# Attention and a gated MLP on one core: a list schedule for the opening only, later chunks emitted in a loop over inner tiles

## The chip, the cores and the metric

The kernel runs on 1 core of one Trainium2 chip. A core has five engines that work side by side, each through its own queue in order: PE (TensorE: matrix products), DVE (VectorE), ACT (ScalarE), POOL (GpSimd) and SP (SyncE, here only for starting transfers). PEld is PE's loading of weights, which overlaps its products. ACT and POOL start transfers too, from their own queues. The metric is the device time of one execution in microseconds (us), the median of several runs. The profile adds the span of one profiled execution, and the clock that PE was granted, as a share of full speed.

## The reference

Two stages, all in float32. The first is attention over 8 batches x 8 heads x 576 positions x 64: a coarse part (q, k and v averaged over groups of 4 positions, full attention over the 144 averages, each result used 4 times) plus a local part (each position sees the 7 positions at a distance under 4). The second is RMS-norm and a gated MLP over the 4608 tokens of 512 values.

```python
q_d, k_d, v_d = (t.reshape(B, H, S // 4, 4, D).mean(axis=3) for t in (q, k, v))
out_up = np.repeat(sm_attn(q_d, k_d, v_d), 4, axis=2)

mask = np.abs(pos[:, None] - pos[None, :]) < 4
scores = np.where(mask, scale * np.matmul(q, k.transpose(0, 1, 3, 2)), -1000000000.0)
out_local = np.matmul(softmax(scores), v)

x = (out_up + out_local).transpose(0, 2, 1, 3).reshape(4608, 512)
xn = x / np.sqrt(np.mean(x * x, axis=-1, keepdims=True) + 1e-06) * rms_g
g = xn @ w_gate                                  # 512 -> 1536
out = (g / (1 + np.exp(-g)) * (xn @ w_val)) @ w_out   # 1536 -> 512
```

## The kernel before

**Tiles and stages.** The 4608 tokens are cut into 18 chunks of 256 (`c`, `NCH`), each as two tiles of 128 (`j`); a token is one position of one batch, its 512 values are 8 heads x 64. The inner width 1536 is cut into 12 inner tiles of 128 (`f`, `NF`). Three classes hold the work.

`Coarse` is one step of the coarse attention: a pair of heads of one batch, 32 steps in all. PE makes the scores (L462), DVE takes their maximum (L471), ACT the exponentials (L481), PE turns them (L490), ACT copies, PE multiplies by the values (L504), DVE scales, and a transfer puts the result into DRAM. The sums over 4 positions behind it are made by `Sums` with accumulating transfers: SP fetches the first quarter, POOL issues three that add the others, for `qk` and for `vs` (L352).

`Attention(c)` is the local attention of chunk c, up to the operand of the MLP. Eight score products of 896 columns, each with a sum (DVE, L669 and L673), a softmax over 7 places (the exponential on ACT, L696; the rest on DVE, L700 to L707), eight value products whose 7 places are shared out among ACT (L716), DVE and POOL (both L723), and their sums (DVE, L742). Then the coarse results are fetched (`load_up`, transfers from ACT's queue) and added, ACT squares and sums (L767), PE makes the mean (L774), DVE starts an inverse root, POOL makes three Newton rounds of four instructions on 128x8 values (L799 to L802), and DVE multiplies (`norm`, L806). Last comes what this document calls the turn: PE transposes (L818, 4 for each half of the chunk), ACT copies the result as `xh` (L822), and DVE takes the remainder as `xl` (L826). `xh` and `xl` are the high and low halves of x, so that three fast products stand for one of float32.

`Forward(c)` is the MLP of a chunk. For each f: 24 first products (L870; 12 for the gate, 12 for the value, each xh and xl against high and low weights that stay in the core's memory), a tanh (ACT, L877), `gate` and `product` (DVE, L880 and L885), the high half `hs` of the result (ACT, L891) and its low half (`low`, L894), and two inner tiles later (`LAG`) 6 second products of 512 columns (L905). At the end of a chunk ACT copies two output tiles (L912) and SP stores them.

**What sets the order.** `Plan` is a list scheduler that runs while the program is built. Each piece of work is a task with an engine, an estimated cost, a due time (`due[c]` is when chunk c is to begin) and the buffers that it uses. Again and again it takes the engine that can begin first, and among the tasks that this engine could begin by then the one with the earliest due time, and emits it. Coarse steps are spread out over three stretches of time by due times. Some tasks have two engines to choose from; `low` is one:

```python
low = task(
    (("DVE", 0.42, soon), ("POOL", 0.95, soon)), 0, lambda e, f=f: self.low(f, e), soon, [high], uses=[sil, hs],
)
```

The plan's own clock goes to the end of the kernel. Up to 270 us of it the order of emission is the order of the program, word for word (`manual_schedule`); what is emitted later is put in order once more by the framework's own scheduler, with the order of emission as its priority.

```python
plan.start()
with tc.manual_schedule():
    plan.run(270.0)
plan.run()
```

**The opening.** Until the first MLP can begin, the core loads and splits the weights (`decode`, on SP, ACT, POOL and DVE), makes eight coarse steps and the attention of chunks 0 and 1, whose value sums go to PE. Eight more coarse steps follow from `due[1] + 10` on, due 18.4 us apart on the plan's clock.

Of the kernel before, what the change touches and what calls it, by code (L numbers as in the profile page):

```python
# [167 lines left out]
def attn_moe_kernel(  # L168
# [135 lines left out]
    def load_second(f):  # L304
# [19 lines left out]
    class Sums:  # L324


        def __init__(self, b, half, at):
# [97 lines left out]
    class Coarse:  # L425


        def __init__(self, b, hp, at, pool=None, tag="ps_a", after=()):
# [22 lines left out]
            stored[b, hp] = task("ACT", 0.06, self.store, at, [scaled], uses=[og], lag=2.2)  # L451

        def scores(self):
# [375 lines left out]
    class Forward:  # L829


        def __init__(self, att, weights, second_weights):
# [132 lines left out]
    def first_weights(f):  # L965
# [12 lines left out]
    atts = [Attention(0, 1, 2, (ps_o, "ps_o"), "DVE")]
    atts.append(Attention(
        1, 2, 2, (ps_a, "ps_a"), "DVE", [h.valued for h in opening] + atts[0].turns,  # L980
    ))
    for p_, (t0, t1) in enumerate(((due[1] + 10, due[4] - 30), (due[4], due[9] - 35), (due[9], due[13] - 35))):
        n = 2 * KT * (p_ + 1)
        for i, it in enumerate(coarse[n:n + 2 * KT]):
            Coarse(*it, t0 + (t1 - t0) * i / 7, after=atts[1].added if p_ == 0 else ())
    for c in range(2, NCH):
        atts.append(Attention(c))
# [83 lines left out]
```

## Time and profile before

| | |
|---|---|
| median of 3 runs | 1203.33 us (1202.26 to 1211.03) |
| the profiled execution | 1203.4 us |
| its span in the trace | 1201.6 us |
| mean granted clock of PE in it | 0.962 |
| first product of chunk 0 | 106.5 us after the span's start |

Each row of the page's first part gives an engine's busy time, its share of the span and its instructions. A row of the windows gives, after the stretch and its length, each engine's busy time in it with the number of its instructions, the granted clock, the busy share of the transfer engines and what they moved. In the timeline and the chain of waits stand the time of the start in us, the duration, the engine, what it made, the line and how many instructions were put together; what follows in square brackets is how long the engine had stood idle ahead of it and who released it. In the table of waits stand PE's instruction, the arrow to the instruction that it waited for, and then the sum, the number and the longest of these waits.

The costliest groups of instructions on PE and on DVE, with busy time and mean duration (ns), then the idle time ahead of them and what ended most of it (products overlap on PE, so the mean of one is longer than the time from one to the next):

```profile
L870 PE MATMUL ps_h<-xh,wg 128*128 128x256 f32 x1728 | 357.4, 289 | 5.0 <-DVE sil L885 2.0
L673 DVE TENSOR_REDUCE sc<-prod 128x14 f32<-128x896 f32 x144 | 153.9, 1076 | 0.6
```

### The profile page before, as it was taken

The numbers are of one execution on the slowest core, as the hardware profiler recorded it, in microseconds if no ns is written. First come the engines' busy times: TensorE is split into PE (matmuls) and PEld (weight loads), VectorE is DVE, ScalarE is ACT, GpSimd is POOL, SyncE is SP. The second block draws the span as 40 slices with busy tenths as digits, with TensorE's granted clock in tenths as the row PEclk, the third lists the DMA queues.
The fourth block names the chain that finished last, engine by engine and source line by source line (L and its number), as shares of the span: only waits on it lengthen the run. The fifth ranks groups of instructions, "written<-read, shape, count | busy, mean of one in ns | idle before, by whom it ended". The sixth has DMA issues, their size and how long they took to land. (4 is left out here: it accounts for less than half of the span.)

```text
span 1201.6 us, 22370 instructions
## 1 busy us (share of the span) xinstructions
PE 1117.7 (93%) x8002; PEld 1021.3 (85%) x8002; DVE 894.0 (74%) x1638; ACT 628.2 (52%) x2284; POOL 370.1 (31%) x590
## 2 busy tenths in 40 slices
PE   5875799999799889999899999999999999999998
PEld 4774688888688788989889998989999999999997
DVE  6786898787884879798796388989585978983232
ACT  1664663747454737557274274664555564672121
POOL 1653451334232233324322234241212222242000
PEclk8866799999899999999999999999999999999999
DMA  9985382446365244263524234543040313300000
GB/s 264 301 281 152 83 207 70 91 94 134 90 126 102 76 93 118 66 137 77 132 55 115 39 91 102 127 88 95 26 111 25 106 52 88 98 12 18 1 18 19
DMA packets 76816, 119.59 MB, mean 100 GB/s; under 512 B 26784, under 2 KB 36256, under 8 KB 76704
## 3 DMA queue, kind: packets, MB, share of 16 engines
q1 hardware_dynamic: 47520, 97.34, 27.7%
q0 software_dynamic: 8640, 15.93, 8.9%
q10 hardware_dynamic: 20544, 4.89, 1.9%
q8 instruction: 63, 1.03, 0.4%
q14 instruction: 49, 0.40, 0.1%
HBM read 106.33 MB, written 11.80 MB: 98 GB/s over the span
## 5 line engine op out<-in xcount | busy, mean ns | idle before, releaser
L905 PE MATMUL ps_o<-wo,hs 128*128 128x512 f32 x1296 | 361.4, 403 | 20.8 <-POOL hs L894 13.2
L870 PE MATMUL ps_h<-xh,wg 128*128 128x256 f32 x1728 | 357.4, 289 | 5.0 <-DVE sil L885 2.0
L870 PE MATMUL ps_h<-xh,wv 128*128 128x256 f32 x1728 | 348.1, 286 | 6.5 <-DVE sil L880 3.9
L870 PEld LDWEIGHTS ps_h<-xh,wg 128*128 128x128 f32 x1728 | 288.9, 194 | 18.2 <-DVE sil L885 3.4
L870 PEld LDWEIGHTS ps_h<-xh,wv 128*128 128x128 f32 x1728 | 283.9, 192 | 16.5 <-DVE sil L880 6.1
L716 ACT ACTIVATE prod<-kv,sc 128x64 f32<-128x64 f32 x1072 | 282.9, 404 | 19.6 <-DVE sc L707 9.8
L905 PEld LDWEIGHTS ps_o<-wo,hs 128*128 128x128 f32 x1296 | 225.8, 192 | 59.3 <-POOL hs L894 15.8
L870 PE MATMUL ps_h<-xl,wg 128*128 128x256 f32 x864 | 247.2, 286 | 0.3 <-DVE xl L826 0.2
L870 PE MATMUL ps_h<-xl,wv 128*128 128x256 f32 x864 | 245.1, 284 | 0.0
L894 POOL TENSOR_TENSOR hs<-sil,hs 128x256 fp32r<-128x256 f32 x124 | 109.7, 896 | 263.3 <-ACT hs L891 250.9
L877 ACT ACTIVATE sil<-ps_h 128x256 f32<-128x256 f32 x216 | 82.3, 381 | 206.4 <-PE ps_h L870 150.6
L891 ACT ACTIVATE hs<-sil 128x256 fp32r<-128x256 f32 x216 | 87.8, 413 | 190.6 <-DVE sil L885 180.8
L870 PEld LDWEIGHTS ps_h<-xl,wg 128*128 128x128 f32 x864 | 167.8, 194 | 5.5 <-DVE xl L826 1.0
L870 PEld LDWEIGHTS ps_h<-xl,wv 128*128 128x128 f32 x864 | 166.0, 192 | 3.9
L669 DVE TENSOR_TENSOR prod<-q_t,kv 128x896 f32<-128x896 f32 x140 | 156.3, 1123 | 5.6 <-DMA q_t<-in_q_band_dram 5.2
L723 POOL TENSOR_TENSOR prod<-sc,kv 128x256 f32<-128x256 f32 x144 | 113.8, 822 | 141.6 <-DVE x_t L742 100.5
L742 DVE TENSOR_REDUCE x_t<-prod 128x128 f32<-128x896 f32 x128 | 137.4, 1078 | 26.7 <-POOL prod L723 12.2
L880 DVE SCALAR_TENSOR_TENSOR sil<-sil,ps_h 128x256 f32<-128x256 f32 x216 | 89.4, 414 | 87.5 <-ACT sil L877 45.0
L673 DVE TENSOR_REDUCE sc<-prod 128x14 f32<-128x896 f32 x144 | 153.9, 1076 | 0.6
L885 DVE SCALAR_TENSOR_TENSOR sil<-sil,ps_h 128x256 f32<-128x256 f32 x216 | 89.3, 416 | 78.6 <-PE ps_h L870 77.7
L723 DVE TENSOR_TENSOR prod<-sc,kv 128x128 f32<-128x128 f32 (+2 forms) x144 | 70.8, 516 | 1.4 <-DMA kv<-in_v_pad_dram 0.5
L352 POOL DMA_DIRECT2D qk<-in_qk_sum_dram x36 | 32.4, 901 | 118.1 <-DMA qk<-in_qk_sum_dram 88.7
(118 smaller groups left out, 1034.3 us busy)
## 6 DMA issues: line engine op xcount, KB each, us to landing
kv<-in_k_pad_dram SPq DMA_DIRECT2D x72, 320.0 KB
kv<-in_v_pad_dram SPq DMA_DIRECT2D x72, 320.0 KB
qk<-in_qk_sum_dram POOLq DMA_DIRECT2D x36, 288.0 KB, 4.6
out_dram<-o_sb SPq DMA_DIRECT2D x36, 256.0 KB
q_t<-in_q_band_dram SPq DMA_DIRECT2D x70, 128.0 KB
vs<-in_v_sum_dram POOLq DMA_DIRECT2D x36, 144.0 KB, 3.7
qk<-in_qk_sum_dram SPq DMA_DIRECT2D x12, 288.0 KB
wo<-in_qk_sum_dram SPq DMA_DIRECT2D x2, 1152.0 KB
```

The costliest lines, as they stand in the source:

```text
L669: nc.vector.tensor_tensor(out=pr, in0=bcast(q[:, s0:s0 + 2], 2, NO), in1=window(k, s0), op=ALU.mult)
L673: nc.vector.tensor_reduce(out=self.sc[:, j, par, s0:s0 + 2], in_=self.pr[i], axis=AX.X, op=ALU.add,)
L716: nc.scalar.activation(out=self.pr[i][:, o, s], in_=self.v[j, par][:, s0 + s + o], func=AF.Copy, scale=p[:, s, o:o + 1],)
L723: (nc.vector if engine == "DVE" else nc.gpsimd).tensor_tensor(out=self.pr[i][:, a:b], in0=bcast(p[:, :, a:b].rearrange("p s o -> p o s"), ...
L742: nc.vector.tensor_reduce(out=self.x[j][:, s0:s0 + 2, par], in_=pr.rearrange("p o s d -> p s d o"), axis=AX.X, op=ALU.add,)
L870: nc.tensor.matmul(out=self.p[f][:, t], lhsT=wi(f)[:, 0, k], rhs=xi[:, k], start=(n == 0), stop=(n == 3 * KT - 1),)
L877: nc.scalar.activation(out=self.sil[f], in_=self.p[f][:, 0], func=AF.Tanh, scale=0.5)
L880: nc.vector.scalar_tensor_tensor(out=self.sil[f], in0=self.sil[f], scalar=1.0, in1=self.p[f][:, 0], op0=ALU.add, op1=ALU.mult,)
L885: nc.vector.scalar_tensor_tensor(out=self.sil[f], in0=self.sil[f], scalar=0.5, in1=self.p[f][:, 1], op0=ALU.mult, op1=ALU.mult,)
L891: nc.scalar.activation(out=self.hs[f][:, 0], in_=self.sil[f], func=AF.Copy)
L894: (nc.gpsimd if engine == "POOL" else nc.vector).tensor_tensor(out=self.hs[f][:, 1], in0=self.sil[f], in1=self.hs[f][:, 0], op=ALU.subtract,)
L905: nc.tensor.matmul(out=self.o[j], lhsT=lhs[:, cols], rhs=rhs(f)[:, 0], start=(f == 0 and i == 0), stop=(f == NF - 1 and i == 2),)
```

## The change

**Three numbers.** `FIRST` = 3, `EARLY` = 7, `COARSE` = {3: 1}. The plan now holds only the opening's tasks: the attention of chunks 0 to 3, the MLP of chunks 0 to 2, the splitting of the weights, and after the first eight coarse steps only `EARLY` = 7 more, due 14 us apart from `due[1] + 10` on. It runs under `manual_schedule` until `due[3] + 10` = 247 us of its own clock.

**A loop for the rest.** The constructors that made tasks are now methods `plan`, and next to them stand methods that emit the same instructions without the plan: `emit(f)` and `emit_second(f)` of `Forward`, `steps()` of `Attention` and of `Coarse`. For chunks 3 to 17 a loop runs over f. Each round emits the inner tile's first products and what follows on ACT and DVE, then the second products of two inner tiles earlier, then those steps of chunk c+1's attention and of the next coarse steps whose place (a number between 0 and 12, in inner tiles) has come. There are two coarse steps to a chunk, in chunk 3 one, until all 32 are made. What the loop emits is ordered once more by the framework's scheduler.

```diff
+        def emit(self, f):
+            self.first(f, 0)
+            self.first(f, 1)
+            self.tanh(f)
+            self.gate(f)
+            self.product(f)
+            self.high(f)
+            self.low(f, "DVE")
+
+        def emit_second(self, f):
+            self.second(f)
+            if f == NF - 1:
+                for j in range(2):
+                    self.copy(j)
+                    self.store(j)
```

So `low` goes to DVE throughout from chunk 3 on; in the plan's chunks it still has its choice. The places of the attention steps (each function emits the lines named above; `root` goes from the mean to `norm`):

```diff
+            todo = [(0.37 * i, lambda i=i: score(i)) for i in range(8)] + [(3.0, softmax)]
+            todo += [(3.1 + 0.42 * i, lambda i=i: value(i)) for i in range(8)]
+            todo += [(at, lambda j=j: add(j)) for j, at in enumerate((4.8, 6.4))]
+            return todo + [(6.5, root), (10.4, lambda: turn(0)), (10.5, lambda: turn(1))]
```

A coarse step is emitted in two parts, `low` (the sums' transfers where they are due, the scores to the exponentials) and `high` (the turning to the store), 1.2 inner tiles apart:

```diff
     plan.start()
     with tc.manual_schedule():
-        plan.run(270.0)
+        plan.run(due[FIRST] + 10)
     plan.run()
+    att, late = atts[FIRST], []
+    for c in range(FIRST, NCH):
+        todo = []
+        if c + 1 < NCH:
+            nxt = Attention(c + 1)
+            todo = nxt.steps()
+            n = min(COARSE.get(c, 2), len(coarse) - done)
+            for i, it in enumerate(coarse[done:done + n]):
+                at = 0.2 + 5.0 * i / n
+                todo += zip((at + 0.1, at + 1.3), Coarse(*it).steps())
+            done += n
+            todo.sort(key=lambda t: t[0])
+        fwd = Forward(att)
+        for f in range(NF):
+            fwd.emit(f)
+            late.append((fwd, f))
+            if len(late) > LAG:
+                fw, g = late.pop(0)
+                fw.emit_second(g)
+            while todo and todo[0][0] < f + 1:
+                todo.pop(0)[1]()
+        att = nxt
+    for fw, g in late:
+        fw.emit_second(g)
```

**Two buffers instead of three.** `m_g` and `z_g`, the maxima and sums of a coarse step, 16 bytes in each of the 72 partitions that they use:

```diff
-            self.m = glob.tile([HALF, 2, 2], FP32, name="m_g", bufs=3)
-            self.z = glob.tile([HALF, 2, 2], FP32, name="z_g", bufs=3)
+            self.m = glob.tile([HALF, 2, 2], FP32, name="m_g")
+            self.z = glob.tile([HALF, 2, 2], FP32, name="z_g")
```

The pools behind, and in them the tiles `xh`, `xl`, `sil`, `hs` and `o_sb`, begin 64 bytes lower in each partition than before.

**What the program's order shows.** The instructions are the same in number and kind on PE, ACT and SP. On POOL they go from 590 to 485 and on DVE from 1638 to 1743: 104 are `low` (on POOL 124 before and 20 now), one is the split of a weight. The coarse steps whose scores stand between the first products of chunks 3 to 16 were 3, 2, 1, 2, 1, 2, 2, 2, 2.5, 0.5, 0, 0, 0, 0 (a step may be cut by a border) and are 2, 1.5, then seven times 2, then 0; in chunks 0 to 2 they were 1, 2, 3 and are 0, 4, 2.5.

The first place is the turn from chunk 2 to chunk 3, where `xh` and `xl` of chunk 3 are made (L822 and L826 before, L910 and L914 now). On ACT there stood before:

```order
L891 ACTIVATE hs<-sil 128x256 x3
L696 ACTIVATE sc<-sc 128x112
L912 COPY o_sb<-ps_o 128x512
L716 ACTIVATE prod<-kv,sc 128x64 x7
L912 COPY o_sb<-ps_o 128x512
L716 ACTIVATE prod<-kv,sc 128x64 x6
L822 CAST xh<-ps_a 128x4x128
L716 ACTIVATE prod<-kv,sc 128x64 x2
L822 CAST xh<-ps_a 128x4x128
```

And now, with L996 the high half `hs`, L784 the exponential of the softmax and L1017 the output copy:

```order
L982 ACTIVATE sil<-ps_h 128x256 x2
L996 ACTIVATE hs<-sil 128x256 x2
L910 CAST xh<-ps_a 128x4x128
L996 ACTIVATE hs<-sil 128x256
L910 CAST xh<-ps_a 128x4x128
L784 ACTIVATE sc<-sc 128x112
L1017 COPY o_sb<-ps_o 128x512 x2
```

The softmax of chunk 4, its value products and the output copies of chunk 2 stood ahead of `xh` and now stand behind it. At the same place on DVE, from the norm of chunk 3 (L806) to its `xl`, before:

```order
L806 TENSOR_TENSOR x_t<-x_t,rinv 128x512 x2
L700 TENSOR_REDUCE z_b<-sc 128x16
L703 TENSOR_SCALAR z_b<-z_b 128x16
L704 RECIPROCAL z_b<-z_b 128x16
L707 TENSOR_TENSOR sc<-sc,z_b 128x112
L723 TENSOR_TENSOR prod<-sc,kv 128x128 x2
L471 TENSOR_REDUCE m_g<-ps_a 72x2
L742 TENSOR_REDUCE x_t<-prod 128x2x64
L723 TENSOR_TENSOR prod<-sc,kv 128x128
L826 TENSOR_TENSOR xl<-ps_a,xh 128x4x128 x2
```

And now (L894 is the norm, L999 the low half on DVE, L761 the sum of a score product, L771 to L781 the softmax's beginning, L508 the maximum of a coarse step):

```order
L894 TENSOR_TENSOR x_t<-x_t,rinv 128x512 x2
L761 TENSOR_REDUCE sc<-prod 128x14
L990 SCALAR_TENSOR_TENSOR sil<-sil,ps_h 128x256
L999 TENSOR_TENSOR hs<-sil,hs 128x256
L771 TENSOR_TENSOR sc<-sc,min_sb 128x56
L778 TENSOR_REDUCE m_b<-sc 128x16
L914 TENSOR_TENSOR xl<-ps_a,xh 128x4x128
L781 TENSOR_TENSOR sc<-sc,m_b 128x112
L508 TENSOR_REDUCE m_g<-ps_a 72x2
L999 TENSOR_TENSOR hs<-sil,hs 128x256
L914 TENSOR_TENSOR xl<-ps_a,xh 128x4x128
```

The end of chunk 4's softmax and its first value work stood between norm and `xl`; now it is the beginning of the softmax, with two low halves of chunk 2. On PE, between the transposes and the next chunk's first product, there are now 6 second products and half of a coarse step's scores at this turn, the half of a step alone at the turn into chunk 4, and 24 first and 6 second products at each of the 13 turns after it. Before, the work at that place was different at each turn, from one coarse step's scores (into chunk 4) to over 200 products (into chunks 8 and 17). Into chunk 4 the mean now stands more than two inner tiles' products further ahead of the transposes than before.

The second place is POOL in one of the even chunks, from the value products to Newton's rounds. Before (L352 is an accumulating transfer of `Sums`, L894 a low half):

```order
L894 TENSOR_TENSOR hs<-sil,hs 128x256 x2
L352 DMA qk<-in_qk_sum_dram 128x576
L723 TENSOR_TENSOR prod<-sc,kv 128x2x128 x2
L352 DMA qk<-in_qk_sum_dram 128x576 x2
L723 TENSOR_TENSOR prod<-sc,kv 128x2x128
L894 TENSOR_TENSOR hs<-sil,hs 128x256 x2
L352 DMA vs<-in_v_sum_dram 72x512
L894 TENSOR_TENSOR hs<-sil,hs 128x256
L352 DMA vs<-in_v_sum_dram 72x512 x2
L799 TENSOR_TENSOR newton<-rinv 128x8
```

And now (L811 is the value product, L362 the accumulating transfer, L887 to L890 a round of Newton's):

```order
L811 TENSOR_TENSOR prod<-sc,kv 128x2x128 x6
L362 DMA qk<-in_qk_sum_dram 128x576 x3
L362 DMA vs<-in_v_sum_dram 72x512 x2
L887 TENSOR_TENSOR newton<-rinv 128x8
L888 TENSOR_TENSOR newton<-newton,rms 128x8
L889 TENSOR_SCALAR newton<-newton 128x8
L890 TENSOR_TENSOR rinv<-rinv,newton 128x8
L887 TENSOR_TENSOR newton<-rinv 128x8
L362 DMA vs<-in_v_sum_dram 72x512
L888 TENSOR_TENSOR newton<-newton,rms 128x8
L811 TENSOR_TENSOR prod<-sc,kv 128x2x128 x2
```

The low halves are gone from POOL; a transfer and the last two value products now stand within Newton's rounds.

More of the change, by code (lines that the diff above doesn't have):

```diff
@@ L308, in attn_moe_kernel @@
     plan = Plan({
-        "qk": 2, "vs": 2, "a_g": 4, "o_g": 2, "m_g": 3, "z_g": 3, "kv": 4, "q_t": 2, "prod": 2, "sc": 2, "x_t": 2,
+        "qk": 2, "vs": 2, "a_g": 4, "o_g": 2, "m_g": 2, "z_g": 2, "kv": 4, "q_t": 2, "prod": 2, "sc": 2, "x_t": 2,
         "up_t": 2, "xh": 2, "xl": 2, "sil": 3, "hs": LAG + 1, "o_sb": W_BUFS, "ps_h": 3, "ps_o": 2, "ps_a": 3,
@@ L324, in attn_moe_kernel, with __init__ @@
     class Sums:
[L327 removed]
+        def __init__(self, b, half, at=None):
             self.b, self.half = b, half
+            if at is None:
+                self.load_qk()
+                self.load_vs()
+                for j in range(1, FAC):
+                    for i in range(2):
+                        self.more(i, j)
+                return
             self.qk_buf, self.vs_buf = buf("qk"), buf("vs")
@@ L425, in attn_moe_kernel, with __init__, steps, low @@
     class Coarse:
-        def __init__(self, b, hp, at, pool=None, tag="ps_a", after=()):
+        def __init__(self, b, hp, pool=None, tag="ps_a"):
             self.b, self.hp, self.pool, self.tag = b, hp, pool or ps_a, tag
+        def steps(self):
+            def low():
+                if (self.b, self.hp // 2) not in sums:
+                    sums[self.b, self.hp // 2] = Sums(self.b, self.hp // 2)
+                self.sums = sums[self.b, self.hp // 2]
+                self.scores()
+                self.peak(0)
+                self.peak(1)
+                self.scale()
+                self.powers(0)
+                self.powers(1)
+            def high():
+                self.invert()
+                for par in range(2):
+                    self.turn(par)
+                    self.copy(par)
+                self.values()
+                self.scaled()
+                self.store()
+            return low, high
+        def plan(self, at, after=()):
+            b, hp, tag = self.b, self.hp, self.tag
             if (b, hp // 2) not in sums:
@@ L975, in attn_moe_kernel @@
     opening = [
-        Coarse(*it, 15.0 + 4.0 * n, *((ps_h, "ps_h") if n // 2 % 2 else (ps_a, "ps_a"))) for n, it in enumerate(coarse[:2 * KT])
-    ]
[L978 to L987, printed above, removed]
+        Coarse(*it, *((ps_h, "ps_h") if n // 2 % 2 else (ps_a, "ps_a"))).plan(15.0 + 4.0 * n)
+        for n, it in enumerate(coarse[:2 * KT])
+    ]
+    atts = [Attention(0, 1, 2, (ps_o, "ps_o")).plan("DVE")]
+    atts.append(Attention(1, 2, 2, (ps_a, "ps_a")).plan("DVE", [h.valued for h in opening] + atts[0].turns))
+    done = 2 * KT
+    for i, it in enumerate(coarse[done:done + EARLY]):
+        Coarse(*it).plan(due[1] + 10 + 14.0 * i, atts[1].added)
+    done += EARLY
+    atts += [Attention(c).plan() for c in range(2, FIRST + 1)]
     for n in range(len(pieces)):
```

63 lines of the change are left out of this document (54 added, 9 removed).

## The prediction

> **What bounds the kernel now.** I read the page first, then cut the span into its 18 chunks: the window bounds are the starts of the 1st, 289th, 577th, ... of the 5184 matmuls of line L870 (288 to a chunk).
>
> ```profile
> PE 1117.7 (93%) x8002; PEld 1021.3 (85%) x8002; DVE 894.0 (74%) x1638; ACT 628.2 (52%) x2284; POOL 370.1 (31%) x590
> ```
> ```profile
> core 0: us, PE busy (x) PEld busy (x) DVE busy (x) ACT busy (x) POOL busy (x), PEclk, DMA share, GB/s
> 106.50:191.60 85.10, 74.75 (x490) 67.49 (x490) 72.88 (x115) 49.17 (x120) 39.44 (x42) 0.90 0.56 137
> 191.60:256.10 64.50, 62.05 (x461) 56.22 (x459) 52.08 (x98) 35.95 (x138) 20.56 (x33) 0.97 0.40 97
> 256.10:327.80 71.70, 62.87 (x443) 55.61 (x441) 57.53 (x109) 40.22 (x152) 22.28 (x36) 0.96 0.41 101
> 327.80:399.60 71.80, 65.70 (x471) 58.96 (x470) 49.60 (x97) 35.05 (x144) 21.89 (x37) 0.95 0.51 104
> 399.60:462.90 63.30, 57.46 (x420) 52.46 (x420) 52.56 (x95) 38.80 (x155) 22.21 (x38) 0.97 0.40 96
> 462.90:516.70 53.80, 53.80 (x404) 50.51 (x403) 45.58 (x83) 33.96 (x138) 18.15 (x32) 1.00 0.35 91
> 579.60:639.80 60.20, 57.53 (x405) 52.51 (x404) 51.02 (x89) 28.98 (x105) 17.82 (x30) 0.97 0.33 86
> 931.80:984.20 52.40, 52.36 (x372) 49.08 (x371) 43.65 (x77) 31.38 (x118) 15.53 (x30) 1.00 0.26 74
> 1090.30:1142.50 52.20, 52.20 (x372) 49.11 (x371) 15.97 (x39) 11.08 (x27) 5.32 (x16) 1.00 0.03 11
> ```
>
> The reader is to see that PE sets the pace, but not evenly: chunks 13 and 16 take 52.4 and 52.2 us, chunks 2 and 3 take 71.7 and 71.8, with the granted clock below 1. To tell work from loss I price what PE must do in a chunk.
>
> ```profile
> 982.94 7.19 PE ps_h L870 x60
> 939.43 2.75 PE ps_o L905 x12
> ```
> ```profile
> 286.55 0.71 PE L462 MATMUL ps_a<-qk 64*72 64x144 f32 x8
> 320.25 1.15 PE L818 MATMUL ps_a<-ident_sb,x_t 128*128 128x128 f32 x8
> 334.16 0.66 PE L490 MATMUL ps_a<-ident_sb,a_g 72*72 72x72 f32 x8
> 339.35 1.19 PE L504 MATMUL ps_a<-vs,a_g 72*72 72x64 f32 x16
> ```
>
> The first two rows are of the chain of waits, the others of the timeline. A first product costs 7.19 / 60 = 0.12 us and a second product 2.75 / 12 = 0.23. A chunk is 288 x 0.12 + 72 x 0.23 = 51.1, plus 1.3 for its transposes and its mean: 52.4 us, which is what chunk 13 takes. A coarse step adds 0.71 + 0.66 + 1.19, taken as 2.5 us. Counting the coarse steps that the old order puts between the chunk starts, chunks 1 to 4 hold 59.0 + 58.4 + 60.2 + 54.4 = 232.0 us of PE work and last 271.3 (191.6 to 462.9): 39.3 are lost. Chunks 5 to 12 hold 453.4 and last 468.9 (462.9 to 931.8): 15.5 lost. Chunks 13 to 16 lose about 1. So what the change can win after the opening lies in chunks 1 to 4.
>
> ```profile
> PE ps_o L905 <- POOL hs L894: 7.1, 6, 1.9
> PE ps_a L462 <- DVE xl L826: 4.7, 1, 4.7
> PE ps_o L905 <- ACT hs L891: 3.5, 2, 2.2
> PE ps_a L818 <- DVE x_t L806: 3.2, 1, 3.2
> ```
> ```profile
> PE ps_o L905 <- POOL hs L894: 6.2, 5, 2.7
> ```
>
> These are PE's longest waits in 191.6 to 462.9 (18.5 us), and its longest in 462.9 to 931.8. The clock column gives the rest: 0.03 x 64.5 + 0.04 x 71.7 + 0.05 x 71.8 + 0.03 x 63.3 = 10.3 us of lost clock in chunks 1 to 4.
>
> **Part 1: the low halves leave POOL.** From chunk 3 on `low` always goes to DVE. The order counts 104 of them moved (124 to 20 on POOL, 92 to 196 on DVE); nothing else but one weight split changes engine, and all DMAs stay in number.
>
> ```profile
> L885 DVE SCALAR_TENSOR_TENSOR sil<-sil,ps_h 128x256 f32<-128x256 f32 x122 | 50.3, 415 | 26.3 <-PE ps_h L870 25.9
> L894 DVE TENSOR_TENSOR hs<-sil,hs 128x256 fp32r<-128x256 f32 x42 | 18.1, 430 | 3.1 <-ACT hs L891 3.1
> ```
> ```profile
> L894 POOL TENSOR_TENSOR hs<-sil,hs 128x256 fp32r<-128x256 f32 x80 | 70.8, 892 | 158.3 <-ACT hs L891 149.9 <-PE ps_a L490 4.6 <-issue 2.6
> L723 POOL TENSOR_TENSOR prod<-sc,kv 128x256 f32<-128x256 f32 x83 | 63.5, 798 | 92.5 <-DVE x_t L742 65.3 <-DVE sc L707 6.7 <-ACT xh L822 5.8
> L352 POOL DMA_DIRECT2D vs<-in_v_sum_dram x16 | 13.7, 858 | 61.9 <-DMA vs<-in_v_sum_dram 41.9 <-PE ps_a L774 8.3 <-PE ps_h L870 3.3
> ```
>
> DVE takes on 104 x 0.43 = 45 us, some 3 per chunk. That is costed at nothing because DVE is busy 45.6 to 57.5 us of chunks that last 53.8 to 71.8; without that idle time the 3 us would be paid in each of 15 chunks. What goes is PE's wait for POOL's low halves, which stand behind products of 0.80 us and accumulating DMAs that wait for one another (41.9 / 16 = 2.6 us each). In their place a low half now stands behind DVE's sums of about 1.1 us, so I do not take all of it: 7.1 falls to 2.4 in chunks 1 to 4, -4.7 (the list still chooses the engine in the first two of these), and 6.2 to 1.7 in chunks 5 to 12, -4.5. PE's wait for ACT's high half goes from 3.5 to 2.0, -1.5. Ends: 0 to -13.3 for POOL's and 0 to -3.5 for ACT's.
>
> The row L894 on DVE also prices a rule that speaks against this step. The Trainium skill (SBUF — State Buffer, section SBUF: two separate sides) says that DVE and GpSimd share a port pair as an exclusive lock: a DVE instruction with two SBUF inputs and a GpSimd one that reads SBUF exclude each other for a whole instruction. Here `low` reads two SBUF tiles, while L885 beside it reads PSUM, and the two differ by 15 ns only, so the trace shows little of it; by the rule at its worst the sum would be that of the second rival below.
>
> **Part 2: the turn from chunk to chunk.** Between chunk 2 and 3 PE stopped because the new x was not split in time:
>
> ```profile
> 321.33 0.71 PE L462 MATMUL ps_a<-qk 64*72 64x144 f32 x4
> 326.70 1.20 PE L462 MATMUL ps_a<-qk 64*72 64x144 f32 x4 [4.67 <-DVE xl L826]
> ```
> ```profile
> 323.81 1.59 ACT L716 ACTIVATE prod<-kv,sc 128x64 f32<-128x64 f32 x6
> 325.25 0.58 ACT L822 CAST xh<-ps_a 128x512 fp32r<-128x512 f32 x1
> ```
> ```profile
> 326.83 0.69 DVE L826 TENSOR_TENSOR xl<-ps_a,xh 128x512 fp32r<-128x512 f32 x1 [0.28 <-ACT xh L822]
> ```
> ```profile
> 327.83:331.90 4.07, 4.07 (x20) 4.07 (x20) 4.01 (x7) 4.07 (x20) 1.00 (x1) 0.50 0.53 153
> ```
>
> The transposes end at 321.4, but ACT works through 13 value products and two output copies before `xh`, and DVE through the next chunk's softmax and value work before `xl`: 6.1 us until 327.5. Then 4.07 us run at half clock, 2.0 more lost. In the new order (the first place in the part on the change) `xh` follows the high halves at once, one `xl` stands six rows behind the norm, and between the transposes and the next chunk lie six second products of 0.23 and half of a coarse step's scores (0.71 / 2): 1.7 us. The floor for transposes to `xl` is in chunk 0:
>
> ```profile
> 103.68 2.14 PE L818 MATMUL ps_a<-ident_sb,x_t 128*128 128x128 f32 x8 [4.49 <-DVE x_t L806]
> ```
> ```profile
> 105.77 1.39 DVE L826 TENSOR_TENSOR xl<-ps_a,xh 128x512 fp32r<-128x512 f32 x2
> ```
>
> 105.82 to 107.16 is 1.3 us. With 1.7 us of PE work in between I leave 1.0 of the 4.7: -3.7. Into chunk 4 the mean now stands 13.8 us of PE work ahead of the transposes (4.1 before), so the 3.2 us wait for the norm goes; but only half of a step's scores, 0.4 us, follows the transposes, and 1.5 is late there next: -1.7. Of the 22.7 us that all PE's waits in chunks 1 to 4 come to, 11.6 go; the clock follows in about that share, -4.7 of 10.3 (ends 0 and -10.3).
>
> **Part 3: the even chunks.** From chunk 5 on the new order has the same pattern at each of 13 turns: after the transposes 24 first and 6 second products, 24 x 0.12 + 6 x 0.23 = 4.3 us. Before, it was 4.4 to 34.8. 4.3 covers 1.3 more than three times over, yet DVE has two sums of 1.1 us just ahead of `xl`, so I charge 0.2 us a turn, 1.6 in chunks 5 to 12 and 1.0 in 13 to 17 (ends 0 and the fourth case). PE's work in chunks 5 to 12 becomes 7 x 57.4 + 52.4 = 454.2, +0.8. Their lost clock (0.03 x 60.2 is the row of chunk 7, and chunk 9 shows the same 0.97: 3.5 in all) gives -2. In chunks 1 to 4 the work changes by 0.1.
>
> On POOL one accumulation of `vs` and two value products now stand among Newton's twelve steps, so Newton waits up to 2.6 + 0.86 + 2 x 0.80 = 5.1 us longer. Behind it on DVE wait the norm, then a low half and a gate. PE has 16.8 us of work between mean and transposes, which hides it. SP's loads keep their order by buffer; ACT issues the same four `up` loads per chunk behind its high halves.
>
> **Part 4: the opening, and 64 bytes.** `m_g` and `z_g` have two buffers instead of three, so the last coarse steps of the opening overlap by two.
>
> ```profile
> 73.13 0.66 PE L462 MATMUL ps_h<-xl 64*72 64x144 f32 x8
> 98.59 0.60 PE L774 MATMUL ps_a<-ss,same_sb 128*128 128x8 f32 x2 [13.03 <-ACT up_t L767]
> ```
>
> PE's 13.03 us wait hangs on the eighth step, begun at 73.13. In the new order the sixth and seventh begin later, but with less of DVE's other work among them: DVE's rows up to the last `o_g` are as many. I take 0, with -4 and +5 as ends (5 is about half of what one step takes). The 64 bytes by which `xh`, `xl`, `sil`, `hs` and `o_sb` move change no instruction's shape; no row of before prices an address, so I take 0, with ends of 5 ns either way per first product, 5184 x 0.005 = 26 us, of which I carry a tenth.
>
> **The sum.** -4.7 - 1.5 - 3.7 - 1.7 - 4.7 (chunks 1 to 4: -16.3), -4.5 - 2.0 + 1.6 + 0.8 (5 to 12: -4.1), +1.0, 0: -19.4. The profiled execution took 1203.4 us, 1.8 over its span and 0.1 from the median of 1203.33, so the time is 1184.0 us, 1.6% less.
>
> **The rivals.** First, more is won: no stop in the turns and a full clock, so that 27 of the 39.3 and 9 of the 15.5 go. 1203.4 - 36 = 1167. For it: chunk 5 already ran with no idle time and clock 1.00. Against: chunks 3 and 4 still turn with 1.7 and 0.4 us of cover.
> Second, DVE takes over POOL's fault: each of eight POOL products in a chunk holds a low half for its 0.80 us, 6.4 us a chunk, and PE waits for DVE as it did for POOL. Then parts 1 and the clock give nothing, and 3.7 + 1.7 is all: 1198. For it: DVE is the busiest engine after PE; against it the 15 ns. This is the port rule's case.
> Third, the order does not change what PE meets (turn stops merely move): 1203, hardly likely, as the rows moved are those that waited.
> Fourth, slower: the turn starves. If transposes to `xl` took 6.1 us at the 13 even turns, as at 327, PE would stop 6.1 - 4.3 = 1.8 us and lose 2.0 of clock each time: 13 x 3.8 = 49, 1233. It decides from 5.8 us on (13 x 1.5 = 19.4). Before, 34.8 us of cover hid such delays; against it, no value product stands ahead of `xh` any more.
>
> **Chances.** The forecast (1177 to 1191) 0.38, the first rival 0.22, the second 0.24, the third 0.05, the fourth 0.11. A measurement of this kernel tells about 1% from no change, so faster means under 1191.3 and slower over 1215.4: faster 0.60, same 0.28, slower 0.12, the last with a long opening. The range 1160 to 1214 leaves out a fourth of the first rival and nearly all of the fourth.
>
> **What would show it.** Right: PE's wait for POOL's `hs` nearly gone, chunks 2 and 3 near 64 us each, chunks 5 to 11 alike at 58 to 59, 12 to 16 at 52.5 to 53, the clock at 1.00 from chunk 4 on. Wrong: PE waiting for `xl` at every turn (fourth), for DVE's `hs` (second), or a first product of chunk 0 later than 111 us.

## The result, and the profile after

The changed kernel takes 1159.0 us (median of 4 runs, 1152.65 to 1160.9) beside 1206.4 us of the kernel before on the same chip: 0.960 of it, with a 95% interval of 0.954 to 0.965. It is faster by 4.0%, where 1.6% was forecast, and it lies 1 us under the low end of the forecast's range (1160). The profiled execution took 1157.7 us, with a span of 1155.9.

The page's first part of the changed kernel, to be held against the row of before:

```profile
PE 1083.4 (94%) x8002; PEld 989.4 (86%) x8002; DVE 912.5 (79%) x1743; ACT 621.3 (54%) x2284; POOL 298.5 (26%) x485
```

PE makes the same 8002 products in 34.3 us less busy time (1117.7 before). A wait that goes shortens the span and not this busy time; a clock that comes back shortens both, but only 10.3 us were lost to the clock in chunks 1 to 4. So a part of the 34.3 must come from something other than the order. The windows of the changed kernel, cut at its own chunk starts (columns as in the prediction), show where:

```profile
192.60:256.76 64.16, 60.34 (x470) 53.17 (x468) 50.81 (x96) 35.85 (x139) 21.18 (x36) 1.00 0.43 99
256.76:321.27 64.51, 61.13 (x467) 54.80 (x466) 57.19 (x106) 36.13 (x140) 22.55 (x36) 1.00 0.59 131
321.27:381.80 60.53, 58.26 (x437) 53.26 (x435) 52.83 (x106) 37.52 (x148) 16.75 (x29) 1.00 0.42 98
381.80:437.85 56.05, 55.17 (x419) 51.54 (x420) 46.23 (x89) 31.64 (x126) 13.60 (x26) 0.97 0.46 108
...
554.33:612.92 58.59, 57.47 (x435) 52.57 (x434) 47.20 (x97) 32.85 (x131) 13.55 (x26) 1.00 0.42 99
...
787.70:844.89 57.19, 57.19 (x435) 52.65 (x434) 47.72 (x98) 33.48 (x130) 9.29 (x20) 1.00 0.25 70
...
946.78:997.72 50.94, 50.94 (x371) 47.88 (x370) 45.10 (x85) 28.92 (x110) 10.59 (x20) 1.00 0.27 76
...
1048.67:1099.23 50.56, 50.56 (x371) 47.52 (x370) 26.51 (x57) 22.12 (x81) 5.64 (x16) 1.00 0.03 11
```

Look at chunks 14 and 16 (the last two rows). PE has no gap there and the clock is 1.00, and yet they take 50.9 and 50.6 us. Chunk 16 of before had no gap, the clock at 1.00 and hardly any other engine at work, and took 52.2. The floor itself has come down. Chunks 2 and 3 went from 71.7 and 71.8 us to 64.5 and 60.5, and the clock is whole there now.

The lower floor is seen in the chain of waits of the changed kernel (start, duration, engine, what, number of products):

```profile
846.67 6.48 PE ps_h L975 x57
```

6.48 / 57 = 0.114 us for a first product, where before it was 7.19 / 60 = 0.120. PE's longest waits in chunks 1 to 4 (192.6 to 437.8; sum, number, longest):

```profile
PE ps_o L1010 <- POOL hs L999: 2.5, 3, 1.2
PE ps_a L906 <- DVE x_t L894: 2.1, 4, 0.9
PE ps_h L975 <- ACT xh L910: 1.7, 1, 1.7
```

And in chunks 5 to 12, its only one:

```profile
PE ps_o L1010 <- DVE hs L999: 5.3, 4, 1.5
```

POOL's low halves, ACT's high halves and the two stops in the turns are gone or small. The longest stop left in a turn is the 1.7 us for `xh` into chunk 4, the only one of the chunks shown whose clock is below 1.00 (0.97). But behind chunk 4 a wait for DVE's `hs` stands where the wait for POOL's stood (6.2 us).

The turn into chunk 3, in the timelines of PE, ACT and DVE of the changed kernel:

```profile
317.73 1.09 PE L906 MATMUL ps_a<-ident_sb,x_t 128*128 128x128 f32 x7
318.75 0.71 PE L499 MATMUL ps_a<-qk 64*72 64x144 f32 x4
319.76 1.67 PE L1010 MATMUL ps_o<-wo,hs 128*128 128x512 f32 x6 [0.30 <-DVE hs L999]
321.27 0.52 PE L975 MATMUL ps_h<-xh,wg 128*128 128x256 f32 x3
```
```profile
319.73 0.57 ACT L910 CAST xh<-ps_a 128x512 fp32r<-128x512 f32 x1
```
```profile
321.54 0.68 DVE L914 TENSOR_TENSOR xl<-ps_a,xh 128x512 fp32r<-128x512 f32 x1
```

The second half of `xh` follows 0.9 us after the transposes and `xl` is done at 322.2, 3.4 us after them (6.1 before). PE hardly stands still meanwhile (0.30 us, for a low half): it makes second products, then three first products that need `xh` alone, then scores.

### The profile page after: what moved, and what is told of

It is laid out like the page before. It is cut to its first block, busy times and chain, and to the rows that moved or that the text cites. A ratio compares the mean times of both kernels' runs of the same rounds, so it can differ in the third digit from the quotient of the medians.

```text
span 1155.9 us, 22258 instructions
## 1 busy us (share of the span) xinstructions
PE 1083.4 (94%) x8002; PEld 989.4 (86%) x8002; DVE 912.5 (79%) x1743; ACT 621.3 (54%) x2284; POOL 298.5 (26%) x485
## 5 line engine op out<-in xcount | busy, mean ns | idle before, releaser
L975 PE MATMUL ps_h<-xh,wg 128*128 128x256 f32 x1728 | 351.5, 284 | 5.2 <-ACT xh L910 2.4
L975 PE MATMUL ps_h<-xh,wv 128*128 128x256 f32 x1728 | 340.7, 280 | 3.2 <-DVE sil L985 3.1
L975 PEld LDWEIGHTS ps_h<-xh,wg 128*128 128x128 f32 x1728 | 285.4, 191 | 15.3 <-ACT xh L910 3.1
L804 ACT ACTIVATE prod<-kv,sc 128x64 f32<-128x64 f32 x1072 | 282.6, 409 | 16.9 <-DVE sc L795 13.6
L975 PEld LDWEIGHTS ps_h<-xh,wv 128*128 128x128 f32 x1728 | 280.2, 189 | 9.5 <-DVE sil L985 5.7
L1010 PEld LDWEIGHTS ps_o<-wo,hs 128*128 128x128 f32 x1296 | 221.6, 189 | 49.6 <-DVE hs L999 9.0
L975 PE MATMUL ps_h<-xl,wv 128*128 128x256 f32 x864 | 240.9, 279 | 0.0
L811 POOL TENSOR_TENSOR prod<-sc,kv 128x256 f32<-128x256 f32 x144 | 115.7, 834 | 215.9 <-DVE x_t L830 75.5
L996 ACT ACTIVATE hs<-sil 128x256 fp32r<-128x256 f32 x216 | 89.4, 416 | 149.5 <-DVE sil L990 136.5
L975 PEld LDWEIGHTS ps_h<-xl,wv 128*128 128x128 f32 x864 | 163.2, 189 | 2.0
L757 DVE TENSOR_TENSOR prod<-q_t,kv 128x896 f32<-128x896 f32 x140 | 151.7, 1085 | 6.3 <-DMA q_t<-in_q_band_dram 5.3
L761 DVE TENSOR_REDUCE sc<-prod 128x14 f32<-128x896 f32 x144 | 154.4, 1076 | 0.4
L830 DVE TENSOR_REDUCE x_t<-prod 128x128 f32<-128x896 f32 x128 | 136.7, 1077 | 20.4 <-ACT prod L804 14.7
L999 DVE TENSOR_TENSOR hs<-sil,hs 128x256 fp32r<-128x256 f32 x196 | 88.2, 450 | 29.7 <-ACT hs L996 29.6
L362 POOL DMA_DIRECT2D qk<-in_qk_sum_dram x36 | 32.3, 896 | 181.8 <-DMA qk<-in_qk_sum_dram 156.2
L811 DVE TENSOR_TENSOR prod<-sc,kv 128x128 f32<-128x128 f32 (+2 forms) x144 | 73.9, 543 | 1.4 <-PE ps_o L826 0.3
```

The costliest lines, as they stand in the source:

```text
L757: nc.vector.tensor_tensor(out=pr, in0=bcast(q[:, s0:s0 + 2], 2, NO), in1=window(k, s0), op=ALU.mult)
L761: nc.vector.tensor_reduce(out=self.sc[:, j, par, s0:s0 + 2], in_=self.pr[i], axis=AX.X, op=ALU.add,)
L804: nc.scalar.activation(out=self.pr[i][:, o, s], in_=self.v[j, par][:, s0 + s + o], func=AF.Copy, scale=p[:, s, o:o + 1],)
L811: (nc.vector if engine == "DVE" else nc.gpsimd).tensor_tensor(out=self.pr[i][:, a:b], in0=bcast(p[:, :, a:b].rearrange("p s o -> p o s"), ...
L830: nc.vector.tensor_reduce(out=self.x[j][:, s0:s0 + 2, par], in_=pr.rearrange("p o s d -> p s d o"), axis=AX.X, op=ALU.add,)
L975: nc.tensor.matmul(out=self.p[f][:, t], lhsT=wi(f)[:, 0, k], rhs=xi[:, k], start=(n == 0), stop=(n == 3 * KT - 1),)
```

## The experiments

The pace of the products and the new order had to be told apart first. Below, "pace" is the mean time from the start of one first product (or second product) to the next matmul's start in chunks 5 to 16, leaving out starts over 140 ns (260 ns) apart: some 1,700 first and 400 second products for each parity of the chunk. "Offset" is where `xh` and `xl` start in the partition, less where the weights start, with multiples of 512 bytes left out; the blocks that one product reads are 512 and 1024 bytes long and lie one behind the other, so a kernel has one offset. It is 0 in the kernel before and -64 in the changed one.

**1. The changed kernel, addresses as before.**

```diff
+    gap = ctx.enter_context(tc.tile_pool(name="gap", bufs=1))
+    gap.tile([P, 16], FP32, name="gap")
     xp = ctx.enter_context(tc.tile_pool(name="xp", bufs=2))
```

> The changed kernel with a gap of 64 bytes ahead of xh, so that xh, xl, sil, hs and o_sb lie where they lay before the change (at multiples of 128 bytes); the order of every engine is the same as in the changed kernel. Theory A (the address sets the pace of PE's products): the time from one first product to the next goes back from 114.5 to 120 ns, chunks 13 to 16 take 52.4 us again instead of 50.9, and the whole is about 18 x 1.45 = 26 us slower than the changed kernel, some 1184 us, 0.982 of before. Theory B (the pace comes from the new order, as fewer POOL instructions read the same memory): 114.5 ns stays, 1158 us.

1173.95 us, 0.976 of before (0.973 to 0.979), and the first products are back at 119.3 ns. A whole chunk without a gap shows it in the windows:

```profile
961.66:1013.77 52.11, 52.11 (x371) 48.95 (x370) 45.15 (x85) 28.85 (x111) 9.43 (x20) 1.00 0.27 74
```

Theory A holds for the pace. The total is 10 us under its number: the address is worth 16 us here (1174.0 beside 1158.2 of run 3, on the same chip), not 26. This run has the new order alone, and it won 29.5 us by the medians (25.3 by the traces), where 19.4 were forecast. PE's busy time in it is 1107.3 us: of the 34.3 us above, 10.4 came with the order and 23.9 with the address. Its windows of chunks 1 to 4, 5 to 12 and 13 to 17, and PE's one wait in chunks 5 to 12:

```profile
191.74:441.57 249.83, 240.34 (x1790) 218.35 (x1788) 205.34 (x393) 141.77 (x555) 74.72 (x127) 0.99 0.47 107
441.57:909.55 467.98, 462.04 (x3410) 424.52 (x3408) 378.02 (x759) 263.85 (x1024) 95.54 (x191) 1.00 0.36 87
909.55:1176.35 266.80, 262.54 (x1853) 246.01 (x1851) 177.33 (x344) 120.25 (x437) 33.86 (x76) 1.00 0.16 48
```
```profile
PE ps_o L1012 <- DVE hs L1001: 5.9, 5, 1.9
```

**2. The kernel before, 64 bytes higher.** The same three lines in the kernel before.

> The kernel before with a gap of 64 bytes ahead of xh, so that xh, xl, sil, hs and o_sb start 64 bytes past a multiple of 128, as in the changed kernel, but 128 bytes higher than there; order unchanged. Theory A: 114 to 115 ns per first product, chunks 13 and 16 at 50.9 us, the whole 26 us faster, 1178 us or 0.978 of before, less what the waits take back. Theory B: 120 ns and 1204 us.

1199.2 us, 0.996 (0.994 to 0.998): between the two theories. The chain of this run has

```profile
975.97 7.07 PE ps_h L872 x60
```

0.118 us for a first product (mean 117.6 ns), but the second products got slower, 233.5 ns after 231.7. 5184 x 1.7 = 8.8 us won and 1296 x 1.8 = 2.3 lost make 6.5; the median shows 4, the interval 2 to 7. So the address works without the new order too, but +64 is not -64: the rule isn't "not on a multiple of 128".

**3. The changed kernel, all of it 64 bytes higher, weights included.**

```diff
     g_sb = const.tile([P, KT], FP32, name="g_sb")
+    const.tile([P, 16], FP32, name="gap")
```

> The changed kernel with a gap of 64 bytes ahead of the weights, so that the weights and all tiles behind them move up together: the weights start 64 bytes past a multiple of 128, xh and xl at a multiple of 128. Theory A1 (what counts is how moving operand and weights lie to each other): 114.5 ns and 1158 us. Theory A2 (what counts is the moving operand's own address): 120 ns and 1184 us. Theory B: 1158 us.

1158.2 us, 0.9625 (0.959 to 0.966), 115.3 ns. `xh` and `xl` lie at the old addresses here, to the byte, and the pace is the new one:

```profile
946.87:997.81 50.94, 50.94 (x372) 47.89 (x370) 45.11 (x85) 28.91 (x110) 10.60 (x20) 1.00 0.28 76
```

So it is the place of the moving operand against the weights that counts.

**4. Only `xh` and `xl` back; `sil`, `hs` and `o_sb` at +64.** A gap of 64 bytes ahead of `xh` as in run 1, and one ahead of the pool that holds `sil`.

> The changed kernel with 64 bytes ahead of xh and 64 more ahead of sil: xh and xl at multiples of 128 bytes as before the change, sil, hs and o_sb 64 past one. If the first products' operand xh and xl is the cause: 120 ns per first product, 230.5 per second product, and about 1182 us. If the cause lies with hs (whose halves are weights of the second products and are written while first products run): 114.5 ns and 1158 us.

1176.3 us, 0.978 (0.974 to 0.981). First products 119.0 ns: `xh` and `xl` carry the effect. A chunk without a gap takes 52.2 us again:

```profile
959.19:1011.36 52.17, 52.17 (x371) 48.86 (x370) 45.20 (x85) 28.83 (x111) 9.43 (x20) 1.00 0.26 74
```

The second products, in which `hs` is the stationary operand and the weights `wo` move, went to 233.8 ns, not 230.5: for them the offset of `hs` counts (230.9 at -64, 231.9 at 0).

**5. Newton's rounds on DVE.** DVE's timeline in the changed kernel shows what the wait in chunks 5 to 9 hangs on:

```profile
539.43 0.43 DVE L990 SCALAR_TENSOR_TENSOR sil<-sil,ps_h 128x256 f32<-128x256 f32 x1
546.62 1.29 DVE L894 TENSOR_TENSOR x_t<-x_t,rinv 128x512 f32<-128x512 f32 x2 [6.76 <-POOL rinv L890]
547.83 0.42 DVE L999 TENSOR_TENSOR hs<-sil,hs 128x256 fp32r<-128x256 f32 x1
```

and POOL's at that time:

```profile
541.16 0.20 POOL L887 TENSOR_TENSOR newton<-rinv 128x8 f32<-128x8 f32 x1
542.75 0.88 POOL L362 DMA_DIRECT2D vs<-in_v_sum_dram  x1 [1.38 <-DMA vs<-in_v_sum_dram]
543.37 0.48 POOL L888 TENSOR_TENSOR newton<-newton,rms 128x8 f32<-128x8 f32 x1
543.54 1.53 POOL L811 TENSOR_TENSOR prod<-sc,kv 128x256 f32<-128x256 f32 x2
```

DVE stands 6.76 us at the norm. Behind it in the queue is a low half, and PE stands 1.51 us for that one:

```profile
548.30 0.97 PE L1010 MATMUL ps_o<-wo,hs 128*128 128x512 f32 x3 [1.51 <-DVE hs L999]
```

```diff
             def root():
                 self.mean()
                 self.rms()
-                self.root("POOL")
+                self.root("DVE")
```

> The changed kernel with Newton's three rounds on DVE (nine instructions) instead of POOL (twelve) from chunk 4 on. In the changed kernel DVE stands at the norm for 5.8 to 7.1 us in chunks 5 to 9, because Newton's rounds stand among POOL's accumulating transfers, and a low half is queued behind the norm: PE then waits 1.1 to 1.9 us for it. Theory A (the fault of POOL has moved to the norm): these waits go, chunks 5 to 9 take 57.2 us as chunks 10 and 11 do, 6 us less in all, 0.955 of before. Rival (DVE has become too full, and every wait for hs is its own work): nine more instructions make it worse, 0.962 or more.

1150.7 us, 0.956 (0.953 to 0.960). Chunks 5 to 12 of this run in one window:

```profile
439.14:890.45 451.31, 451.31 (x3409) 416.06 (x3408) 384.48 (x825) 262.17 (x1013) 74.12 (x94) 1.00 0.37 91
```

PE is busy in all of it: 451.3 us beside 458.0, and nothing is left to win there but products. Theory A holds. The waits that go are 5.3 us in the trace above and 9.3 and 9.2 in two more traces of the changed order at the same offset (runs 3 and 12), where the stage took 461.7 and 464.5 us; so the line is worth 7 to 13 us there. In run 11, which has it too, the stage is 451.6 us without a wait.

**6. Low halves on POOL in the loop.**

```diff
-            self.low(f, "DVE")
+            self.low(f, "POOL")
```

> The changed kernel with all low halves of chunks 3 to 17 on POOL instead of DVE: it undoes part 1 alone. Theory A (leaving POOL was worth several us): PE waits for POOL's hs behind value products and accumulating transfers, two to four times in each of chunks 3 to 11 at 1 to 2.5 us, 20 to 40 us more than the changed kernel, 0.975 to 0.995 of before. Rival (the order of the emission is what helped, the engine of low is hidden by the two inner tiles between): 0.960 as the changed kernel.

1167.1 us, 0.9685 (0.964 to 0.973): about 8 us more than the changed kernel by medians from different chips, less than theory A's 20; the intervals overlap a little (0.954 to 0.965 there). The traces are clearer. PE's only wait in chunks 5 to 12, where the changed order has 5.3 to 9.3 us:

```profile
PE ps_o L1010 <- POOL hs L999: 15.6, 5, 4.0
```

The waits are five in all, not two to four in each chunk: one in each of chunks 5 to 9, which have accumulating transfers on POOL, and none in 10 to 12, where the value products are still there but the transfers are not (in the changed kernel's windows POOL has 26 instructions in chunk 7 and 20 in chunk 11). The wait of 3.97 us in chunk 6, with POOL's rows ahead of it, shows what holds the low halves:

```profile
531.56 0.90 POOL L362 DMA_DIRECT2D qk<-in_qk_sum_dram  x1 [5.60 <-DMA qk<-in_qk_sum_dram]
536.72 0.87 POOL L362 DMA_DIRECT2D qk<-in_qk_sum_dram  x1 [4.26 <-DMA qk<-in_qk_sum_dram]
537.29 1.73 POOL L999 TENSOR_TENSOR hs<-sil,hs 128x256 fp32r<-128x256 f32 x2
```
```profile
538.39 1.80 PE L1010 MATMUL ps_o<-wo,hs 128*128 128x512 f32 x4 [3.97 <-POOL hs L999]
```

ACT had made the high half of the first by 529.1. It is POOL's two idle times between accumulating transfers, 5.60 and 4.26 us, that keep it from the low halves, not the value products.

**7. The turn one inner tile later.** `(10.4, ...turn(0)), (10.5, ...turn(1))` become 11.4 and 11.5.

> The changed kernel with the transposes one inner tile later, so that about 2.7 us of second products and scores stand between transposes and the next chunk instead of 4.1. In the changed kernel xl is ready 3.6 to 3.95 us after the transposes. Theory A (the turn is covered by just enough, as the fourth rival has it with its deciding point at the length of the cover): PE stops about 1.2 us at each of 13 turns, 16 us more, 1174 us. Rival (the 3.9 us are mostly DVE's work of lower urgency, which the scheduler puts behind xl when xl is needed sooner): no stop, 1158 us.

1163.2 us, 0.967 (0.962 to 0.971), 4 us more than the changed kernel, which is not clear of the noise. PE's waits in chunks 5 to 12:

```profile
PE ps_o L1010 <- ACT hs L996: 5.5, 4, 1.6
PE ps_h L975 <- DVE xl L914: 0.2, 1, 0.2
```

It does not stop for `xl` (0.2 us), though at the turns into chunks 5 to 15 the first product now follows the transposes after 2.1 to 3.3 us: theory A falls. The scheduler put `xl` up to 3.9 us behind the transposes again, and first products that need only `xh`, scores and second products fill in. The waits for the low half have become waits for ACT's high half, of much the same sum (5.5 beside 5.3), so no loss at the turn is shown.

**8. Three buffers again in the opening.** `"m_g": 3, "z_g": 3` in the plan, `bufs=3` in memory, and the gap of run 1, which makes the offset +64.

> The changed kernel with three buffers again for the maxima and sums of the coarse steps, in the plan and in memory, and a gap that keeps xh 64 bytes past a multiple of 128 (128 bytes higher than in the changed kernel, as in the second run). Theory A (two buffers made the opening longer): the first product of chunk 0 comes at 106.5 us as before instead of 108 to 111, and 2 to 4 us are won there; the pace is 117.6 ns as in the second run, which costs 14 us against the changed kernel, so 1170 us in all. Rival (the opening differs by the split of the other tasks, not by these buffers): first product at 108 to 111, 1172 us.

1170.5 us, 0.973 (0.968 to 0.977). The first product of chunk 0 comes at 106.0 us, as theory A has it (111.0 in the changed kernel), but chunk 0 then takes longer:

```profile
106.04:191.13 85.09, 73.47 (x482) 66.21 (x483) 70.98 (x116) 48.21 (x119) 39.86 (x42) 0.92 0.56 138
```

It ends at 191.1, in the changed kernel at 192.6 after 81.6 us. Over all traces with the new opening and two buffers (ten of them), the first product of chunk 0 comes at 107.4 to 111.9 us, with three buffers (this run, the kernel before and run 2) at 104.6 to 106.5. But chunk 0 ends at 187.9 to 192.6 with two and at 189.3 to 191.6 with three: what the two buffers cost the opening, chunk 0 gives back.

**9 and 10. Other offsets.** Kernel of run 5 with `xh` and `xl` of even and odd chunks in two pools, and gaps that give each parity an offset of its own.

> The kernel with Newton's rounds on DVE, whose chunks 5 to 16 lose nothing to waits, with other places for xh and xl: in even chunks they start 32 bytes below a multiple of 256 counted from the weights' start (offset -32), in odd chunks 32 above (+32). Known so far: offset 0 119.4 ns per first product, +64 117.6, -64 115.4. Theory A1 (only the offset between moving operand and weights counts): even and odd chunks of this one run differ, even ones lie between 115.4 and 119.4 ns, odd ones between 117.6 and 119.4; a chunk is 0.29 us longer for each ns. Rival (any start that is no multiple of 128 gives the same): even and odd chunks alike.

> The same kernel with offset -128 in even chunks and -96 in odd ones (the maxima and sums of the coarse steps lie behind the output tiles, which makes room). Theory A1 with a period of 256 bytes or more: -128 differs from 0 and is not 119.4 ns; -96 lies near -64's 115.4. With a period of 128 bytes: -128 is as 0, 119.4 ns, and -96 as +32. Rival as in the run before: even and odd chunks alike.

They take 1157.0 and 1162.3 us, one execution each, beside 1202.8 of the kernel before. The windows of an odd and an even chunk (13 and 14; neither has a gap), first of run 9, then of run 10:

```profile
890.50:942.05 51.55, 51.55 (x371) 48.25 (x370) 45.73 (x93) 28.69 (x111) 6.61 (x8) 1.00 0.26 75
942.05:993.98 51.93, 51.93 (x372) 48.66 (x371) 45.89 (x93) 28.55 (x110) 6.66 (x8) 1.00 0.26 74
```
```profile
894.60:946.57 51.97, 51.97 (x372) 48.73 (x370) 45.76 (x93) 28.76 (x111) 6.58 (x8) 1.00 0.26 75
946.57:998.58 52.01, 52.01 (x371) 48.74 (x370) 45.84 (x93) 28.47 (x110) 6.59 (x8) 1.00 0.26 74
```

All the paces that were measured, in ns; for second products the offset is that of `hs` against `wo`:

| offset, bytes | first product | second product | run |
|---|---|---|---|
| -128 | 118.8 | | 10, even chunks |
| -96 | 118.2 | 232.8 | 10, odd chunks |
| -64 | 115.7 | 230.9 | the changed kernel |
| -32 | 118.3 | | 9, even chunks |
| 0 | 119.3 | 231.7 | the kernel before |
| +32 | 116.9 | 233.4 | 9, odd chunks |
| +64 | 117.6 | 233.5 | 2 |

Even and odd chunks of run 9 differ, so the rival (any start off a multiple of 128) falls. -96 and -64 are not alike to +32 and +64, so the period is not 128 bytes. Theory A1 had +32 between 117.6 and 119.4 and -96 near -64: both wrong, the pace is no smooth function of the offset. Of these seven offsets the changed kernel's is the best; whether another is better was not tried. Traces of the same offset agree to 0.4 ns: 119.0 to 119.3 at 0, 115.3 to 115.8 at -64, 117.6 to 117.8 at +64.

Could it be the other engines' tiles, which `xh` may meet or miss? Chunk 17 speaks against that: no attention work is left in it and POOL does nothing, and yet its first products take 119.6 ns at 0 (the kernel before), 117.6 at +64 (run 2) and 114.4 at -64 (the changed kernel).

**11 and 12. Everything that helped, and the changed kernel beside it.** Run 11 takes Newton's rounds on DVE in chunks 2 and 3 too, and all low halves on DVE in the plan.

> The changed kernel with Newton's rounds on DVE for chunks 2 to 17 and every low half on DVE, the plan's chunks included. Theory A (what POOL still holds in chunks 0 to 4 is PE's wait): of PE's waits in chunks 1 to 4, POOL's hs 2.3 and the norm 3.1 us go, chunks 5 to 16 stay at 57.2 and 50.9 as with Newton's rounds on DVE alone; 1145 to 1150 us, 0.951 to 0.956 of before and 6 to 13 us under the changed kernel on the same chip. Rival (the opening is bound by the weights' loading and DVE is its fullest engine, so that more work on DVE there makes chunks 0 to 2 longer): no gain against Newton's rounds alone, 0.956 or more.

> The changed kernel itself, on the same chip and beside the same runs of the kernel before as the run above: 0.960 of before.

Run 11: 1151.45 us, 0.956 (0.952 to 0.960). The changed kernel beside it: 1159.9 us, 0.962 (0.958 to 0.966). Against run 5 nothing more is won: the rival holds. POOL's waits in chunks 1 to 4 have gone and PE waits for DVE there instead:

```profile
PE ps_a L906 <- DVE x_t L894: 3.7, 1, 3.7
PE ps_a L906 <- DVE xl L914: 1.5, 1, 1.5
```

So run 11 is 8.4 us under the changed kernel on the same chip, though the intervals overlap a little. Run 5 was not taken beside the changed kernel, but its ratio of 0.956 is run 11's, so its one line is enough for the difference.

## Why the prediction was wrong

The spans by stage, cut at the chunk starts, in us:

| stage | before | new order alone (run 1) | changed kernel | forecast for the order |
|---|---|---|---|---|
| up to the end of chunk 0 | 191.6 | 191.7 | 192.6 | 0 |
| chunks 1 to 4 | 271.3 | 249.8 | 245.3 | -16.3 |
| chunks 5 to 12 | 468.9 | 468.0 | 458.0 | -4.1 |
| chunks 13 to 17 | 269.8 | 266.8 | 260.0 | +1.0 |
| span | 1201.6 | 1176.3 | 1155.9 | -19.4 |

In these traces the order brought -25.3 and the addresses -20.4. A second pair of traces, both at offset +64 and with three buffers (runs 2 and 8), gives -26.3 for the order: -24.2 in chunks 1 to 4, -0.6 in chunks 5 to 12, -3.3 behind them. By the medians on one chip it is -29.5 for the order and -15.8 for the addresses (1203.45, 1173.95 in run 1, 1158.2 in run 3). So 16 to 20 us come from the addresses. The order alone, at some 1174 us, lies within the forecast's range of 1160 to 1214; the addresses took the kernel out of it.

**The address: the step that failed.** "No row of before prices an address, so I take 0, with ends of 5 ns either way per first product, 5184 x 0.005 = 26 us, of which I carry a tenth." It measured 119.3 - 115.7 = 3.6 ns, 18.7 us, and 0.8 ns for each of 1296 second products, 1.1 us more. The size lies inside the bound of 5 ns. What was wrong was to carry a tenth of it: nothing in the trace of before made 0 likelier than either end, and a cost that falls on 5184 products on the path needs only 2 ns to reach 1% of the time. With the whole bound carried, the range would have begun at 1184 - 26 = 1158 or lower.

**The turn and the clock (part 2): right in kind, too small.** PE's waits in chunks 1 to 4 went from 22.7 us to seven that add up to 9.1 in run 1, -13.6 where -11.6 was forecast. The clock there rose from 0.96 to 0.99: 10.3 us of lost clock became 0.01 x 249.8 = 2.5, -7.8 where -4.7 was forecast. I let the clock follow the waits in proportion; about three quarters of it came back.

**The low halves (part 1): right in chunks 1 to 4, wrong in 5 to 12.** POOL's 7.1 us became 1.6 (forecast 2.4). In chunks 5 to 12, POOL's 6.2 was to become 1.7 of DVE's. It became 5.9 in run 1, and the stage won 0.9 us instead of 4.1. The step that failed is in part 3: "Newton waits up to [...] 5.1 us longer. Behind it on DVE wait the norm, then a low half and a gate. PE has 16.8 us of work between mean and transposes, which hides it." The cover is that of the transposes, but the low half has a nearer reader, the second products two inner tiles later. DVE stood at the norm for 5.8 to 7.1 us in chunks 5 to 9. Run 5 shows it: with Newton off POOL the stage is 451.3 us and has no wait. So the transfers on POOL hold PE whichever engine makes the low half: directly in run 6, through Newton and the norm in the changed kernel.

**Second rival (a lock between DVE and POOL): not seen.** Its sign came, PE waiting for DVE's `hs` (5.3 us), but by the norm's wait for Newton, as run 5 shows. `low` on DVE has a mean of 450 ns in the changed kernel and `product` beside it 416; before it was 430 and 415:

```profile
L999 DVE TENSOR_TENSOR hs<-sil,hs 128x256 fp32r<-128x256 f32 x196 | 88.2, 450 | 29.7 <-ACT hs L996 29.6
L990 DVE SCALAR_TENSOR_TENSOR sil<-sil,ps_h 128x256 f32<-128x256 f32 x216 | 89.8, 416 | 6.3 <-PE ps_h L975 4.3
```

In chunk 17, with POOL idle, they take 425 and 421. What DVE stood idle for ahead of `low` was ACT's `hs`, 29.6 of 29.7 us. POOL still makes eight value products in a chunk, in run 5 too, and in run 5 PE waits for no low half from chunk 5 on. Of the rule of the Trainium skill (SBUF — State Buffer, section SBUF: two separate sides) this trace shows no more than these some 30 ns in the time of `low`.

**First rival (no stop in the turns and a full clock, 1167 us):** of the four its time is the nearest, but not for its reason. The order alone won 25 to 30 us, not its 36; in run 1 PE still lost 9.1 and 5.9 us to waits.

**Fourth rival (the turn starves): not seen.** From the last transpose to `xl` it took 3.2 to 3.95 us at the turns into chunks 6 to 16; the next chunk's first product followed after 3.9 to 4.1, and the first one that reads `xl` after 5.6 to 7.3. Into chunk 5 `xl` took 6.6 us, more than the rival's 5.8, and PE made other products meanwhile and did not stop. The rival counted the cover to the chunk's first product, which reads `xh` alone; run 7 shows that even a shorter cover costs nothing at that place.

**Chunks 13 to 17** were to lose 1.0 and won 3.0 with the order: my charge of 0.2 us a turn was for stops that did not come, and before lost more there (1.6 us of waits, in three `sil` and one `hs`) than I had seen. The rest of the 3.0 is not accounted for. **The opening** came out as forecast, by a different road: chunk 0 began 3 to 4.5 us later and was as much shorter. Its sign of being wrong, a first product later than 111 us, came at 111.03 and cost nothing.

What stays open: why -64 is best and how the table's values come about. The runs show that the offset between what PE streams and the weights it loads decides; which reads meet they do not show. Each offset but 0, -64 and +64 was seen in one run only.

## What to carry to other kernels

Where PE runs without a gap, price its pace, not only its waits: hold the duration of a chunk without gaps against the same chunk of another version, and try two or three placements of the moving operand against the weights before working on the order. A cost that no row prices but that falls on every product of the path belongs into the range whole. And cover has to be counted for everything that is queued behind a waiting instruction, to its nearest reader, not for the result that the wait is about.

## What the hardware showed that was not expected

The pace of fp32 products with a new weight load each changes with the distance in memory between moving operand and weights: 115.7 to 119.3 ns for 256 columns, 230.9 to 233.5 for 512, at a granted clock of 1.00. 64 bytes were worth 16 us by the medians and 20 by the traces, of some 1175, more than half of what the new order won.
